# A linear-attention and MLP kernel: a sixth buffer for the k and q features, and a new order of all operations

## The chip, the cores and the metric

The kernel runs on 1 core of a Trainium2 chip. The metric is the device time of one execution in microseconds (us), the median over several runs. The engines are TensorE (PE; its weight loads are listed as PEld), VectorE (DVE), ScalarE (ACT) and GpSimd (POOL); SyncE (SP) issues the DMA transfers. SBUF is the on-chip memory of the engines, PSUM the banks that TensorE writes into.

## What is computed

Eight batches of eight heads of linear attention feed a token-wise MLP, all in fp32:

```
def phi(x):                                   # (8, 8, 576, 64) -> 256 features
    proj = einsum('bhsd,df->bhsf', x, w_phi)  # w_phi 64 x 128
    proj = proj - max(abs(proj), axis=-1)
    return concatenate([exp(proj), exp(-proj)], axis=-1)
q_p, k_p = phi(q), phi(k)
kv  = einsum('bhsf,bhsd->bhfd', k_p, v)
z   = sum(k_p, axis=2)
num = einsum('bhsf,bhfd->bhsd', q_p, kv)
den = einsum('bhsf,bhf->bhs', q_p, z)[..., None] + 1e-6
x   = (num / den) as 4608 tokens x 512

h  = x @ w_in                                 # 512 -> 1024
e  = exp(h - max(h)); sm = e / (sum(e) + 1e-9)
s  = h * sm
ln = (s - mean(s)) / sqrt(var(s) + 1e-6) * g_ln
out = ln @ w_out                              # 1024 -> 512
```

## The kernel before

**Attention.** There are 16 units u (a batch and four of its heads), each with two sub-visits. For a sub-visit TensorE projects k (`k_rows`, `k_mid`: tiles pjk, op name kp) and q (`q_proj`: tiles pq, three products of high and low halves, op name qp with a 320- and a 256-column part; for units 0 to 2 `q2_rows`, tiles pjq). DVE takes the row maximum of k (km) and subtracts it into a feature tile ek (`k_sub`, ks), and ACT makes exp(x) and exp(-x) of it (`k_exp`, ke). The q side is turned by DVE transposes (qt: blk<-pq), has its maximum taken (qm4), is subtracted on POOL (qs), turned back into a feature tile fq (`q_back`, qb), and made into exponentials by ACT (`q_exp`, qe). `visit` (V) then issues on TensorE the 72 num matmuls of the sub-visit before it and the 80 kv matmuls of its own; ACT copies kv out (kvf), the quotient is made (E, rc, y), and y goes by DMA to a scratch tensor dx.

**Tag e.** The tiles ek (four heads by four token blocks) and fq, and the exponential tiles of the last MLP tiles (`moe_tile`, t > 32), take their room from one tag, `e`, with tiles of 5,120 bytes per partition. `SBUF_BUFS` (lines 40 to 43) says how many tiles a tag has.

**MLP.** 36 token tiles t of 128 tokens go in 18 pairs g. The weights w_in come in four loads (wraw, 1 MB each; `w_load`), are rejoined from their 64-bit form by ACT (whi, op ws) and DVE (wb, wd), split into high and low halves (wb_h, wb_l, wt_h, wt_l), and for w_out also scaled (wg) and copied by ACT (w_out_h, op woh). A pair reads x as xT by four DMAs from dx, POOL makes sums S, ACT and POOL split them (ah, al), TensorE makes four shared products U1 to U4 (`moe_shared`) and three own ones (`moe_h`), each of six matmuls, DVE joins them with a running maximum (nm). Each tile then goes through an exponential, a product, a centring and a square pass (eu; op var is the square) to a DVE transpose, a DMA out and four in (du, uTs), a high copy on ACT (uhs), a low part on POOL (uls), and 24 matmuls o in two halves (`moe_o`), and a copy os that goes out.

**What sets the order.** Nothing is scheduled by a cost when the kernel is built: `SEQUENCE` (lines 55 to 192) is a table of 2,604 operation numbers, `Plan.order` walks it, gives each new tile the buffer of its tag that came free first, and the main loop plays the operations in that order. Each engine runs its own instructions in the order of the table, and so does SP its DMA issues. Every instruction is recorded at line 274, in `InOrder`, so the profile tells operations apart by their tiles. PSUM has six banks of tag a and one pair of tag h.

Of the kernel before, what the change touches and what calls it, by code (L numbers as in the profile page):

```python
# [41 lines left out]
    rk=3, rkm=2, rv=3, m=4, e=5, eh=2, kf=2, qr=2, qh=4, q4=2, m4=2, E=2, rc=2,  # L42
# [13 lines left out]
    120, 3, 121, 4, 76, 110, 124, 87, 177, 78, 20, 95, 0, 122, 88, 200, 77, 125, 96, 111, 79, 89, 83, 80, 81,  # L56
    90, 116, 21, 180, 123, 84, 85, 97, 112, 12, 91, 113, 126, 82, 266, 114, 86, 210, 92, 117, 93, 127, 115, 129,
    8, 94, 128, 206, 130, 98, 131, 166, 102, 99, 100, 106, 118, 103, 119, 135, 101, 132, 104, 181, 201, 16, 107,
    178, 22, 105, 133, 152, 134, 155, 137, 182, 146, 136, 23, 108, 13, 153, 58, 59, 157, 183, 156, 154, 14, 202,
    15, 60, 61, 9, 149, 204, 203, 205, 109, 10, 167, 147, 148, 211, 11, 150, 151, 168, 158, 44, 48, 169, 184,  # L60
    214, 17, 45, 170, 159, 173, 186, 255, 212, 138, 171, 174, 216, 160, 269, 213, 219, 18, 56, 57, 62, 289, 172,
    215, 207, 161, 139, 185, 162, 163, 175, 140, 187, 19, 217, 176, 267, 218, 208, 179, 196, 220, 24, 209, 270,
    221, 192, 256, 34, 141, 271, 64, 222, 164, 193, 290, 46, 25, 188, 189, 225, 291, 197, 223, 242, 47, 165,
    194, 224, 257, 142, 343, 195, 190, 227, 226, 292, 243, 268, 6, 228, 35, 244, 275, 272, 354, 377, 229, 191,
    245, 262, 236, 258, 143, 144, 230, 274, 263, 198, 259, 239, 145, 273, 36, 231, 49, 357, 5, 246, 232, 264,
    293, 294, 260, 247, 276, 265, 261, 237, 199, 29, 240, 63, 241, 50, 233, 234, 238, 285, 281, 51, 282, 305,
    378, 7, 379, 66, 248, 249, 250, 299, 277, 52, 26, 283, 235, 251, 308, 358, 54, 27, 295, 296, 286, 306, 359,
    360, 284, 252, 253, 39, 278, 310, 345, 309, 297, 298, 311, 314, 53, 279, 307, 350, 65, 380, 40, 254, 346,
    55, 312, 1410, 351, 280, 1411, 315, 381, 300, 382, 1412, 316, 1413, 313, 28, 67, 301, 302, 287, 352, 30,
    303, 304, 383, 444, 1414, 401, 317, 327, 318, 1418, 1419, 353, 330, 361, 1415, 1424, 31, 41, 42, 1416, 344,  # L70
    68, 1420, 384, 1426, 385, 1475, 1476, 324, 1434, 1477, 1427, 288, 355, 356, 331, 325, 1478, 333, 1421, 1430,
    1417, 37, 362, 329, 326, 1422, 1425, 1428, 425, 347, 32, 328, 33, 402, 1423, 69, 386, 335, 348, 1483, 349,
    1429, 1435, 1479, 332, 436, 1432, 334, 1437, 387, 437, 438, 1480, 1431, 1438, 1441, 1484, 364, 1433, 70,
    319, 71, 369, 38, 365, 1442, 1439, 1443, 370, 373, 1485, 1446, 1436, 1486, 336, 1481, 1447, 1491, 320, 403,
    371, 1482, 374, 366, 337, 72, 1440, 1458, 526, 1444, 439, 388, 321, 1492, 1493, 1448, 372, 391, 483, 1459,
    1494, 1495, 1460, 1496, 1487, 1449, 1450, 404, 405, 427, 392, 367, 406, 1489, 407, 1451, 389, 1488, 432,
    408, 1499, 440, 363, 368, 390, 1497, 433, 393, 459, 1452, 426, 1500, 322, 323, 409, 441, 375, 43, 74, 338,
    73, 1502, 1490, 434, 1463, 442, 394, 1503, 1453, 1464, 1506, 410, 339, 1465, 443, 395, 518, 376, 428, 446,
    1466, 75, 484, 340, 1467, 1507, 1508, 429, 671, 411, 1454, 430, 341, 1511, 342, 435, 431, 485, 1468, 412,
    1445, 1512, 1504, 396, 1513, 460, 415, 413, 397, 1498, 414, 416, 398, 417, 451, 1455, 452, 461, 1501, 1514,  # L80
    1456, 399, 1469, 455, 1515, 1516, 447, 418, 1470, 400, 486, 419, 420, 1505, 1461, 421, 1509, 541, 462, 422,
    448, 449, 450, 445, 1517, 487, 488, 1471, 423, 456, 424, 463, 465, 1540, 453, 542, 1518, 464, 466, 489, 454,
    1541, 1542, 1543, 543, 1462, 1472, 467, 1519, 1473, 490, 1548, 491, 468, 623, 469, 1523, 492, 507, 470, 473,
    1544, 1549, 471, 1545, 544, 545, 1550, 472, 1546, 547, 1551, 1524, 600, 1520, 1525, 1457, 1554, 1556, 546,
    565, 521, 1547, 548, 1564, 1552, 549, 1605, 550, 1558, 1553, 474, 475, 1606, 1607, 1557, 1510, 1555, 508,
    493, 527, 1528, 1559, 519, 1567, 1560, 1521, 1565, 1608, 1609, 1613, 1529, 1530, 1562, 1531, 522, 1526,
    1522, 1561, 1568, 520, 1614, 1571, 1610, 1563, 1532, 494, 495, 1533, 523, 1572, 1569, 457, 476, 477, 528,
    566, 567, 647, 1573, 590, 509, 458, 589, 497, 1576, 1615, 1621, 496, 1577, 1578, 1611, 514, 478, 1579, 498,
    1580, 1612, 1474, 524, 682, 1616, 1566, 1622, 510, 525, 603, 515, 516, 511, 604, 605, 1623, 551, 499, 1625,
    512, 1624, 513, 533, 517, 1581, 534, 1619, 537, 1534, 1527, 1570, 1626, 1620, 1535, 1588, 1536, 1617, 529,  # L90
    1589, 500, 530, 538, 648, 608, 552, 555, 1590, 649, 568, 553, 1593, 569, 535, 536, 501, 479, 1594, 1618,
    591, 556, 571, 570, 557, 480, 572, 1574, 573, 554, 1629, 1582, 1632, 1575, 764, 574, 1537, 1583, 575, 531,
    481, 532, 1630, 1538, 601, 1633, 602, 1591, 592, 1595, 539, 606, 593, 1636, 1592, 1627, 558, 559, 1637, 560,
    482, 1584, 594, 561, 576, 1596, 1597, 595, 579, 562, 1598, 563, 1638, 577, 1634, 607, 1628, 502, 705, 596,
    578, 580, 540, 597, 624, 564, 1631, 503, 581, 625, 1635, 1599, 1585, 504, 598, 599, 619, 505, 683, 1586,
    1600, 1653, 582, 626, 506, 583, 584, 1641, 1639, 629, 1642, 620, 585, 706, 1654, 1655, 586, 587, 1539, 627,
    628, 588, 1670, 630, 610, 1671, 615, 1672, 631, 1601, 632, 1602, 616, 1673, 707, 617, 611, 612, 1678, 609,
    633, 1603, 729, 613, 650, 651, 652, 673, 1674, 1643, 1679, 685, 653, 1644, 614, 1604, 684, 1675, 1680, 1686,
    1684, 1735, 1658, 1694, 1676, 1687, 634, 635, 637, 654, 655, 1659, 1681, 1690, 678, 1677, 1682, 1656, 638,
    1736, 618, 672, 639, 1645, 1683, 656, 1688, 1697, 1660, 1692, 1689, 1695, 730, 1646, 657, 1685, 679, 1640,  # L100
    1691, 1698, 1661, 686, 687, 636, 690, 1647, 1693, 1648, 621, 1701, 1702, 1699, 708, 1737, 674, 680, 1738,
    1739, 1740, 681, 658, 640, 641, 711, 642, 643, 644, 675, 1743, 661, 1744, 691, 731, 754, 709, 1703, 645,
    662, 663, 1741, 710, 712, 1662, 622, 1663, 713, 1706, 1696, 1749, 659, 660, 1649, 676, 1745, 1746, 714,
    1704, 1705, 1664, 1751, 688, 1650, 1752, 1665, 689, 1742, 677, 1700, 1651, 1753, 1755, 811, 812, 715, 1754,
    1756, 701, 1718, 1719, 646, 813, 1707, 732, 1708, 1709, 1710, 664, 665, 753, 692, 1711, 666, 667, 716, 773,
    1720, 717, 668, 1723, 702, 1750, 1666, 1759, 1721, 1747, 1748, 1724, 1712, 1713, 772, 719, 697, 733, 669,
    693, 720, 694, 755, 721, 698, 735, 1762, 670, 1760, 695, 734, 736, 737, 765, 766, 699, 1667, 756, 1587, 757,
    696, 1725, 700, 1722, 1726, 718, 1727, 1728, 703, 1657, 1763, 1766, 738, 758, 759, 1729, 1730, 760, 722,
    1652, 1757, 723, 787, 1767, 1768, 739, 1771, 1769, 1731, 761, 704, 1772, 767, 1773, 724, 1774, 1758, 1668,
    1669, 740, 741, 835, 1764, 742, 743, 1732, 762, 744, 745, 725, 763, 726, 768, 769, 846, 727, 1761, 847, 770,  # L110
    771, 1765, 788, 783, 789, 790, 728, 746, 1775, 747, 1776, 748, 869, 749, 793, 750, 1770, 751, 1733, 1777,
    784, 752, 1778, 1800, 791, 792, 2, 814, 794, 817, 795, 870, 871, 815, 774, 816, 1714, 1801, 818, 796, 1802,
    797, 1783, 1803, 1808, 1809, 1814, 1804, 849, 1734, 1805, 1784, 1785, 819, 850, 893, 894, 1715, 1806, 1807,
    820, 851, 852, 848, 836, 1779, 1788, 917, 1810, 1816, 1865, 1716, 1866, 1811, 1867, 1868, 1786, 821, 1780,
    1781, 1824, 779, 1817, 780, 798, 801, 775, 776, 802, 1818, 1789, 1869, 1812, 1870, 1827, 799, 872, 875,
# [1202 lines left out]
```

## Time and profile before

| | us |
|---|---|
| three runs | 637.32, 641.12, 640.41 |
| median | 640.41 |
| profiled execution | 634.97 |
| its span on the core | 633.2 |

The profiled execution lies 5.44 us under the median of the runs. Its span is divided below into windows of 20 us; the busy time of an engine in a window is the time in which it had an instruction in execution. In the timelines each row gives the start, the duration, the engine, the tiles (out<-in) and the number of instructions put together; brackets hold the idle time before and what ended it.

### The profile page before, as it was taken

To read this page: it belongs to the slowest core of one execution; us is meant where nothing else is said; L and a number is where in the kernel's file an instruction comes from. 1 tells how busy PE (TensorE), PEld (TensorE's weight loads), DVE (VectorE), ACT (ScalarE), POOL (GpSimd) and SP (SyncE) were. 2 spreads that over 40 slices of the span, in tenths; PEclk is the share of its full clock that TensorE was granted. 3 is DMA by queue.
4 is the path that set the end of the run, shared out by engine and by line. 5 is a ranking of instruction groups with operands and counts; after the bars stand their busy time and mean duration, and the time that the engine had idled before them with its cause. 6 is when DMAs were issued, how large, how long until landed. Compare 5 with 4: busy or idle time off the path is not lost.

```text
span 633.2 us, 19010 instructions
## 1 busy us (share of the span) xinstructions
PE 617.8 (98%) x7558; PEld 525.0 (83%) x7558; DVE 475.3 (75%) x995; ACT 458.1 (72%) x842; POOL 432.0 (68%) x468
## 2 busy tenths in 40 slices
PE   6999899999999999999999999999999999999997
PEld 5988688878888888888888888888888888888887
DVE  6999999787868885877876779988897973453540
ACT  4999798677957877477877667887776686466743
POOL 0568998777658864856786586657876675487732
PEclk9999999999999999999999999999999999999999
DMA  8886354754438374455574627545535355356441
GB/s 282 310 274 206 95 162 165 217 144 158 133 115 228 118 218 146 132 143 129 155 229 158 166 87 227 161 126 194 157 128 145 103 165 182 82 158 182 150 134 67
DMA packets 100200, 103.38 MB, mean 163 GB/s; under 512 B 50448, under 2 KB 73232, under 8 KB 99600
## 3 DMA queue, kind: packets, MB, share of 16 engines
q1 hardware_dynamic: 100112, 102.18, 52.8%
q8 instruction: 59, 0.97, 0.6%
q14 instruction: 29, 0.24, 0.1%
HBM read 64.92 MB, written 37.22 MB: 161 GB/s over the span
## 4 chain that ended last, share of the span: by engine, by line
PE 88%; DVE 6%; ACT 2%; DMA 2%; issue 1%; SPq 0%; ACTq 0%; DVEq 0%
PE o L274 31%; PE U L274 15%; PE h L274 12%; PE num L274 10%; PE kv L274 9%; PE pjk L274 5%; PE pq L274 4%; DVE m L274 2%; DVE w L274 1%; DVE ek L274 1%; PE pjq L274 1%; DVE dq L274 1%; DMA xT<-dx 1%; ACT fq L274 1%; DMA out<-os 1%
## 5 line engine op out<-in xcount | busy, mean ns | idle before, releaser
L274 PE MATMUL o<-w_out_h,uhs 128*128 128x512 f32 x280 | 112.4, 402 | 0.0
L274 POOL TENSOR_TENSOR uls<-uTs,uhs 128x1024 fp32r<-128x1024 f32 x35 | 83.7, 2390 | 41.9 <-ACT uhs L274 28.9
L274 PE MATMUL o<-w_out_l,uhs 128*128 128x512 f32 x280 | 109.4, 391 | 0.0
L274 PE MATMUL o<-w_out_h,uls 128*128 128x512 f32 x280 | 109.2, 390 | 0.0
L274 ACT ACTIVATE ek<-ek 128x512 f32<-128x512 f32 (+1 forms) x160 | 90.6, 584 | 16.9 <-DVE ek L274 16.1
L274 PEld LDWEIGHTS num<-kvf,fq 128*64 128x64 f32 x2304 | 70.0, 138 | 9.6 <-issue 5.0
L274 PE MATMUL kv<-rv,ek 128*64 128x65 f32 x2048 | 76.9, 222 | 0.0
L274 PE MATMUL num<-kvf,fq 128*64 128x65 f32 x2304 | 74.4, 223 | 0.1
L274 POOL TENSOR_TENSOR blk<-blk,m 128x1152 f32<-128x1152 f32 x26 | 55.6, 2138 | 27.3 <-DVE m L274 27.3
L274 ACT ACTIVATE fq<-fq 128x640 f32<-128x640 f32 (+1 forms) x104 | 69.4, 679 | 6.1 <-DVE fq L274 5.6
L274 PEld LDWEIGHTS kv<-rv,ek 128*64 128x64 f32 x2048 | 71.0, 138 | 0.8 <-ACT fq L274 0.2
L274 ACT ACTIVATE eu<-h,nm 128x1024 f32<-128x1024 f32 x36 | 40.1, 1115 | 36.4 <-DVE nm L274 31.7
L274 PEld LDWEIGHTS o<-w_out_h,uhs 128*128 128x128 f32 x280 | 52.6, 188 | 12.5 <-issue 0.2
L274 POOL TENSOR_TENSOR al<-S,ah 128x512 fp32r<-128x512 f32 x36 | 47.5, 1320 | 21.8 <-ACT ah L274 20.9
L274 PEld LDWEIGHTS o<-w_out_h,uls 128*128 128x128 f32 x280 | 52.6, 188 | 11.2
L274 PEld LDWEIGHTS o<-w_out_l,uhs 128*128 128x128 f32 x280 | 52.6, 188 | 10.3
L274 POOL TENSOR_TENSOR y<-E,rc 128x512 f32<-128x512 f32 x64 | 43.6, 704 | 21.3 <-DVE rc L274 19.1
L274 DVE TENSOR_REDUCE m<-pjk 128x4 f32<-128x512 f32 (+1 forms) x80 | 48.9, 620 | 11.4 <-PE pjk L274 11.1
L274 DVE SCALAR_TENSOR_TENSOR eu<-h,eu 128x1024 f32<-128x1024 f32 x36 | 43.8, 1218 | 18.1 <-ACT eu L274 17.7
L274 DVE STREAM_TRANSPOSE ub<-eu 128x1024 f32<-128x1024 f32 x35 | 43.1, 1233 | 14.3 <-ACT eu L274 5.5
L274 DVE STREAM_TRANSPOSE blk<-pq 128x320 f32<-128x320 f32 (+1 forms) x104 | 43.4, 455 | 10.8 <-PE pq L274 10.7
L274 POOL TENSOR_TENSOR lq<-rawq,hq 128x576 fp32r<-128x576 f32 x26 | 37.2, 1432 | 20.9 <-ACT hq L274 20.1
(113 smaller groups left out, 1558.4 us busy)
## 6 DMA issues: line engine op xcount, KB each, us to landing
du<-ub SPq DMA_DIRECT2D x35, 512.0 KB, 3.0
uTs<-du SPq DMA_DIRECT2D x140, 128.0 KB, 3.2
dx<-y SPq DMA_DIRECT2D x32, 288.0 KB, 2.7
out<-os SPq DMA_DIRECT2D x35, 256.0 KB, 3.0
rv<-in_v SPq DMA_DIRECT2D x32, 264.0 KB, 4.1
rawk<-in_k SPq DMA_DIRECT2D x32, 256.0 KB, 4.0
xT<-dx SPq DMA_DIRECT2D x64, 128.0 KB, 3.3
rawq<-in_q SPq DMA_DIRECT2D x26, 288.0 KB, 3.9
```

The lines of the kernel that those rows point to most:

```text
L274: return self.tc.keep_in_program_order(method(*args, **kwargs))
```

## The change

Tag `e` gets six tiles instead of five, and `SEQUENCE` is another order of the same 2,604 operations. No operation is added, taken away or changed. Of the 2,604 places 79 hold the same operation as before; half of the operations stand at most 10 places from where they stood, the farthest 742.

```diff
@@ -39,7 +39,7 @@
 SBUF_BUFS = dict(
-    rk=3, rkm=2, rv=3, m=4, e=5, eh=2, kf=2, qr=2, qh=4, q4=2, m4=2, E=2, rc=2,
+    rk=3, rkm=2, rv=3, m=4, e=6, eh=2, kf=2, qr=2, qh=4, q4=2, m4=2, E=2, rc=2,
     y=1, m2k=2, S=2, A=4, A1=2, c=3, big=6, nm=4, sm=3, ms=2, mv=2, sa=2, sc=3,
 )
@@ -53,142 +53,142 @@
 SEQUENCE = (
-    120, 3, 121, 4, 76, 110, 124, 87, 177, 78, 20, 95, 0, 122, 88, 200, 77, 125, 96, 111, 79, 89, 83, 80, 81,
+    3, 120, 0, 76, 87, 4, 95, 121, 77, 124, 96, 116, 78, 88, 110, 90, 122, 89, 125, 20, 83, 84, 206, 117, 85,
...
```

Walked through, the old table holds five e tiles at a time at 20 of the 131 allocations and never asks for more; the new one holds six at 13 of them, the first time in unit 0.

What the table moves, at four places. **SP at the start**, before:

```order
L274 DMA wph<-in_w_phi 128x256
L274 DMA rawk<-in_k 128x512
L274 DMA rawq_155<-in_q 128x512
L274 DMA rawk<-in_k 128x128 x2
L274 DMA wraw_173<-in_w_in 128x2048
L274 DMA rawk<-in_k 128x512
```

and now, later in its list:

```order
L274 DMA rawq_164<-in_q 128x128
L274 DMA vz_70<-in_v 64x132
L274 DMA rawq_177<-in_q 128x512
L274 DMA vz_70<-in_v 64x132
L274 DMA wraw_186<-in_w_in 128x2048
L274 DMA rawq_192<-in_q 128x128
L274 DMA rawk<-in_k 128x128
```

The load of the fourth w_in block (wraw, the first of the four that ACT uses) was SP's seventh DMA and is its twelfth, behind a q load (rawq_177) that needs a tile which an earlier projection frees. On ACT its copy whi stood second after the two w_phi copies and now stands ninth.

**ACT before the visit of unit 3, second half**, before (the last fq row here is the last feature that this visit's num needs; ek and fq are its k and q exponentials):

```order
L274 ACTIVATE fq<-fq 128x2x320
L274 ACTIVATE ek<-ek 128x4x128
L274 ACTIVATE fq<-fq 128x2x320
L274 ACTIVATE fq<-fq 128x2x256
L274 CAST uhs<-uTs 128x1024
L274 ACTIVATE w_7_1257<-w_7_1257,gcol 128x512 x2
L274 CAST w_out_h<-w_7_1257 128x1024
```

and now:

```order
L274 ACTIVATE fq<-fq 128x2x256
L274 ACTIVATE ek<-ek 128x4x128
L274 CAST w_out_h<-w_7_1261 128x1024
L274 ACTIVATE fq<-fq 128x2x320
L274 ACTIVATE ek<-ek 128x4x128
L274 CAST uhs<-uTs 128x1024
L274 ACTIVATE eu,mv<-eu 128x1024 x2
```

The copy w_out_h of the last weight block, and ahead of these rows its scaling, stood behind the features and now stand ahead of the last two of them; the square pass of tile 0 (eu,mv) has moved from ahead to behind.

**PE at the first product U of pair 4**, before:

```order
L274 MATMUL pq<-hq,w_hh 128x320 x2
L274 MATMUL pq<-hq,w_ll 128x320 x2
L274 MATMUL pq<-lq,w_hh 128x320 x2
L274 MATMUL pjk<-wph,rawk 128x128 x8
L274 MATMUL pjk<-wph,rawk 128x256
L274 MATMUL pq<-hq,w_hh 128x256 x2
L274 MATMUL pq<-hq,w_ll 128x256 x2
L274 MATMUL pq<-lq,w_hh 128x256 x2
L274 MATMUL U<-wb_h,ah 128x512
L274 MATMUL U<-wb_l,ah 128x512
```

and now:

```order
L274 MATMUL o<-w_out_h,uhs 128x512
L274 MATMUL o<-w_out_l,uhs 128x512
L274 MATMUL o<-w_out_h,uls 128x512
L274 MATMUL pjk<-wph,rawk 128x128 x8
L274 MATMUL pq<-hq,w_hh 128x256 x2
L274 MATMUL pq<-hq,w_ll 128x256 x2
L274 MATMUL pq<-lq,w_hh 128x256 x2
L274 MATMUL U<-wb_h,ah 128x512
L274 MATMUL U<-wb_l,ah 128x512
L274 MATMUL U<-wb_h,al 128x512
```

Ahead of U now stand the second half of an o, a projection pjk and one part pq only; the other pq part and the small pjk have moved ahead of that o half.

**PE after the visit of unit 14, second half**, where the q projections of unit 15 stand, before:

```order
L274 MATMUL pq<-hq,w_hh 128x256 x2
L274 MATMUL pq<-hq,w_ll 128x256 x2
L274 MATMUL pq<-lq,w_hh 128x256 x2
L274 MATMUL pq<-hq,w_hh 128x320 x2
L274 MATMUL pq<-hq,w_ll 128x320 x2
L274 MATMUL pq<-lq,w_hh 128x320 x2
L274 MATMUL pjk<-wph,rawk 128x128 x8
L274 MATMUL h<-wt_h_1023,ah 128x512
```

and now:

```order
L274 MATMUL pq<-hq,w_hh 128x320 x2
L274 MATMUL pq<-hq,w_ll 128x320 x2
L274 MATMUL pq<-lq,w_hh 128x320 x2
L274 MATMUL pjk<-wph,rawk 128x128 x8
L274 MATMUL pq<-hq,w_hh 128x256 x2
L274 MATMUL pq<-hq,w_ll 128x256 x2
L274 MATMUL pq<-lq,w_hh 128x256 x2
L274 MATMUL o<-w_out_h,uhs 128x512
```

Before, the 320-column part of unit 15's first sub-visit stood ahead of the visit, its 256-column part behind the visit and the second sub-visit's 320-column part directly behind that. Now both parts of the first sub-visit stand behind the visit with the eight k projections between them, and the second sub-visit's parts come behind the products o of tile 24.

## Rows read from the trace of the kernel before

**Rows 1.** The page: busy time of each engine with its share of the span and its instructions.

```profile
PE 617.8 (98%) x7558; PEld 525.0 (83%) x7558; DVE 475.3 (75%) x995; ACT 458.1 (72%) x842; POOL 432.0 (68%) x468
```

**Rows 2.** Busy time by windows: from:to and length, then for each engine the busy time and (instructions), the granted clock, the share of the DMA engines in use and GB/s.

```profile
0.00:20.00 20.00, 14.45 (x184) 12.31 (x185) 13.87 (x25) 11.30 (x24) 1.24 (x9) 1.00 0.88 307
20.00:40.00 20.00, 19.01 (x400) 16.63 (x400) 19.26 (x31) 18.43 (x40) 14.39 (x10) 1.00 0.78 271
40.00:60.00 20.00, 18.59 (x398) 16.31 (x397) 18.05 (x30) 19.20 (x47) 16.66 (x14) 1.00 0.70 225
60.00:80.00 20.00, 17.84 (x266) 15.04 (x266) 18.88 (x29) 15.27 (x32) 19.82 (x13) 1.00 0.46 121
80.00:100.00 20.00, 20.00 (x337) 17.45 (x334) 17.59 (x36) 19.96 (x36) 18.67 (x15) 1.00 0.50 165
100.00:120.00 20.00, 19.65 (x253) 16.43 (x248) 16.10 (x39) 16.18 (x32) 15.85 (x17) 1.00 0.55 175
120.00:140.00 20.00, 19.05 (x140) 15.21 (x141) 17.70 (x46) 11.53 (x20) 16.70 (x22) 1.00 0.73 192
...
480.00:500.00 20.00, 19.40 (x305) 16.43 (x305) 18.22 (x43) 12.48 (x24) 10.11 (x15) 1.00 0.30 82
...
560.00:580.00 20.00, 20.00 (x90) 16.58 (x89) 9.96 (x18) 12.76 (x19) 16.02 (x20) 1.00 0.58 167
```

**Rows 3.** Waits: the instruction that waited, what it waited for, us in total, times, the longest. First those of PE, then the only one of all engines in which a new ek or fq waited for its buffer.

```profile
PE pjq L274 <- DMA wph<-in_w_phi: 3.8, 1, 3.8
PE U L274 <- DVE blk L274: 2.2, 1, 2.2
...
DVE ek L274 <- PE kv L274: 1.8, 2, 1.6
```

**Rows 4.** The start, timeline of SP's queue: the first and the last of the four loads of w_in blocks (1 MB each).

```profile
3.52 0.44 SPq L274 DMA_DIRECT2D wraw<-in_w_in  x1
...
15.76 0.70 SPq L274 DMA_DIRECT2D wraw<-in_w_in  x1
```

**Rows 5.** The DMA view of the moments 3.5 and 15.7 us: the wraw load issued there, KB, us from issue to landing.

```profile
wraw<-in_w_in SPq DMA_DIRECT2D x1, 1024.0 KB, 7.2
...
wraw<-in_w_in SPq DMA_DIRECT2D x1, 1024.0 KB, 8.7
```

**Rows 6.** The start, timeline of ACT: the copy of the first loaded block, and what stands at the place that is ninth in its list.

```profile
10.74 1.07 ACT L274 ACTIVATE whi<-wraw 128x1024 f32<-128x1024 f32 x1 [0.18 <-DMA wraw<-in_w_in]
...
14.22 0.41 ACT L274 ACTIVATE ek<-ek 128x256 f32<-128x256 f32 x1
```

**Rows 7.** Timelines of PE and of POOL around the first product U.

```profile
68.40 0.47 PE L274 MATMUL U<-wb_h,ah 128*128 128x512 f32 x1 [2.15 <-DVE blk L274]
...
65.09 1.72 POOL L274 TENSOR_TENSOR al<-xT,ah 128x512 fp32r<-128x512 f32 x1
...
69.20 2.21 POOL L274 TENSOR_TENSOR al<-S,ah 128x512 fp32r<-128x512 f32 x1
```

**Rows 8.** Timeline of ACT before and behind the visit of unit 3, second half: square pass, the last features, the scaling and copy of the last weight block, and the last features of the next visit.

```profile
87.16 1.05 ACT L274 ACTIVATE eu<-eu 128x1024 f32<-128x1024 f32 x1
...
93.25 1.25 ACT L274 ACTIVATE fq<-fq 128x640 f32<-128x640 f32 x2
...
95.34 1.34 ACT L274 ACTIVATE w<-w,gcol 128x512 f32<-128x512 f32 x2
96.71 1.05 ACT L274 CAST w_out_h<-w 128x1024 fp32r<-128x1024 f32 x1
...
106.27 2.69 ACT L274 ACTIVATE fq<-fq 128x640 f32<-128x640 f32 x4
```

**Rows 9.** Timeline of PE in the same stretch: the visit's start, the projection behind it, and the next visit's start.

```profile
95.72 2.32 PE L274 MATMUL num<-kvf,fq 128*64 128x65 f32 x72
...
101.14 1.16 PE L274 MATMUL pjk<-wph,rawk 64*128 64x128 f32 x14 [0.35 <-DVE m L274]
...
109.26 1.92 PE L274 MATMUL num<-kvf,fq 128*64 128x65 f32 x58
```

**Rows 10.** Timelines of PE and ACT around the first product U of pair 4.

```profile
191.28 0.41 PE L274 MATMUL pq<-hq,w_hh 64*128 64x320 f32 x2
...
191.82 1.68 PE L274 MATMUL pjk<-wph,rawk 64*128 64x128 f32 x18
193.71 0.39 PE L274 MATMUL pq<-hq,w_hh 64*128 64x256 f32 x2 [0.20 <-ACT os L274]
...
194.26 0.50 PE L274 MATMUL U<-wb_h,ah 128*128 128x512 f32 x1
...
192.45 0.62 ACT L274 CAST ah<-xT 128x512 fp32r<-128x512 f32 x1 [1.56 <-DMA xT<-dx]
```

**Rows 11.** Timeline of PE behind the visit of unit 14, second half.

```profile
486.12 0.78 PE L274 MATMUL pq<-hq,w_hh 64*128 64x256 f32 x2
...
486.75 0.39 PE L274 MATMUL pq<-lq,w_hh 64*128 64x256 f32 x2
487.71 0.42 PE L274 MATMUL pq<-hq,w_hh 64*128 64x320 f32 x2 [0.58 <-DVE c L274]
...
488.26 1.05 PE L274 MATMUL pjk<-wph,rawk 64*128 64x128 f32 x16
489.24 0.50 PE L274 MATMUL h<-wt_h,ah 128*128 128x512 f32 x1
```

270 rows, old and new, of the table SEQUENCE are left out of this document.

## The prediction

> **What bounds the kernel now.** I read the page first: PE is busy for 617.8 of 633.2 us [rows 1], so only 15.4 us of the span are free of TensorE work, and the change neither adds nor removes a matmul. Then the windows, which show where these 15.4 us lie: 5.55 in 0 to 20 us, 0.99, 1.41 and 2.16 in the next three, 0 in 80 to 100, 0.35 and 0.95 up to 140, and 0.60 in 480 to 500 [rows 2]; nearly all of the rest is the fill and drain of the last microseconds. From 0 to 140 that makes 11.4 us. In this first stretch the others are full in turn: DVE 19.26, 18.05 and 18.88 of 20 in the windows from 20 to 80, ACT 19.20 and 19.96 in those from 40 and 80, POOL 19.82 in that from 60 [rows 2]. Behind 140 PE itself is the limit and the others have room, as in 560 to 580 with DVE at 9.96 and ACT at 12.76 [rows 2]. The granted clock is 1.00 in all of these windows, the upper level of 2.4 GHz. Third come the waits: the longest of PE is 3.8 us for w_phi at the start, the next 2.2 before the first U, and only twice, for 1.8 us together, does a new ek wait for a tile of tag e to come free [rows 3].
>
> So the sixth buffer relieves a wait of 1.8 us, on DVE, in a program that TensorE bounds; what the change is worth has to come from the order.
>
> **The change part by part.** The sum is made against the profiled execution, 634.97 us, which is 5.44 under the median of 640.41; I add the sum to the median.
>
> *PE's work.* The same matmuls; fewer changes between kinds of block (2,156 rows in the order instead of 2,161) are nothing I can tell. 0.
>
> *The sixth buffer.* Walked through, it is held at 13 places, so it is used. Its whole price in the trace is 1.8 us of DVE idle [rows 3], in a stretch where DVE is 90 to 96% busy with work that comes afterwards all the same. 0 on PE's path by itself, -1.8 at most.
>
> *The start.* The first w_in load was issued at 3.52 us and landed 7.2 later; ACT's copy of it came at 10.74 and had waited 0.18 for it [rows 4 to 6]. It now stands behind a q load that needs a tile which the first projections free, and ACT's copy is ninth, where ACT stands at 14.22 [rows 6]. An issue at about 7 us, an estimate from those projections (they end near 6), with the 7.2 of the same load gives 14.2: no wait. With the 8.7 of the last load [rows 5] and an issue at 8.9 it would land at 17.6 and ACT would wait 3.4 us; ACT's list runs in order, so its exponentials wait as well. I take 0, since the same block at nearly the same moment has the 7.2; ends 0 and +3.4. POOL's list has room here (1.24 of 20 busy [rows 2]).
>
> *The first U.* Its 2.15 us wait is put down to a DVE transpose that frees a PSUM bank [rows 7]. The new table gives it a bank that an earlier transpose frees. But the product also needs its low part al from POOL, 65.09 to 66.81, and the later products need the next al, which ended at 71.41 and which the table puts behind one more POOL sum; POOL has 0.18 us free in this window [rows 2, 7]. What U gains it is likely to wait for again. 0; ends -1.6 (68.40 less 66.81) and +1.2 (one more sum and its wait).
>
> *80 to 110 us.* ACT is full, 19.96 of 20 [rows 2]. The visit of unit 3, second half, started at 95.72, and the last features it needed first ended at 94.50, a slack of 1.2 [rows 8, 9]. The scaling and the copy of the last weight block, 1.34 and 1.05, now stand ahead of the last of them, and a square pass of 1.05 goes behind: +1.3 against 1.2 of slack, so next to nothing here. Up to the next visit's last features, which ended at 108.96 for a start at 109.26, a slack of 0.3 [rows 8, 9], these moves cancel, but the square pass of the following tile, another 1.05, has come in ahead of them: 1.05 less 0.3 is about +0.7. A wait of PE before a projection (0.35 shown at 101.14, and the block is late by about 1.1 as a whole [rows 9]) goes, because that projection moves behind the o; but a PE that is earlier finds ACT no earlier. I take +0.7; ends -1.1 (only the gain) and +2.0 (both sets of ACT work fall on PE).
>
> *The first U of pair 4.* It hung on xT: ACT's cast waited 1.56 us for the DMA and started at 192.45 [rows 10]. PE spent the time on 18 projections that took 191.82 to 193.71, 1.89 us, where 16 take 0.98 [rows 11] and the two of double width would add a quarter of that; the excess is about 0.66, in which the wait of 0.20 lies [rows 10]. Now half an o stands in that place, and the U comes about 1.85 us of PE work later. -0.7; ends -0.9 and 0. The U's consumers come later too, on DVE and ACT, whose lists have room here.
>
> *Behind unit 14.* The two pq groups back to back took 486.12 to 488.26, and the second waited 0.58 for the bank that a DVE addition frees [rows 11]. Where nothing waits, one group takes 0.54 (191.28 to 191.82 [rows 10]); so 2.14 less 1.08 is 1.06 of excess. With eight projections between them and DVE's transposes done meanwhile I take -1.0; ends -1.06 and 0. DVE is the fullest engine beside PE here, 18.22 of 20 [rows 2], so what could be late next is the row maximum behind those projections; an o of 2.7 us covers it.
>
> *The rest of the table*, 140 to 480 and 500 to 633: pieces of DVE and POOL work move by one to two microseconds against PE, in windows where PE is 20.00 of 20 busy and DVE has two to ten free. 0.
>
> Sum: 0 + 0 + 0 + 0.7 - 0.7 - 1.0 = -1.0. The profiled execution comes to 634.0, the median to **639.4 us**, no change. The ends without the buffer's are -4.7 and +6.6, all of them at once.
>
> **The rivals.** A measurement of this kernel can tell about 1%, 6.4 us, from no change: faster means under 634.0, slower over 646.8.
>
> *The first 140 us open up.* With room for features ahead and a new order, PE's idle time there goes: 11.4 less the 3.8 of the w_phi load, which no buffer shortens, is 7.6 [rows 2, 3]; with -1.7 from the two later places, 640.4 - 9.3 = 631.1 us. For it: the gaps come again and again in this stretch, and the start has been rearranged most. Against it: DVE, ACT and POOL are full in turn, and a buffer makes none of them faster. The Trainium skill (Perfetto Trace Analysis, Optimization Strategy) says that the same gap repeating on the engine that should be saturated can mean that there is not enough SBUF for the next tile; by that rule the 7.6 us would go. Here the trace disagrees: the gaps of PE name w_phi, a transpose and an addition, and the e tile is named for 1.8 us on DVE. Chance 0.18.
>
> *ACT falls behind.* The late first load holds ACT's list for 3.4 us at its ninth place. From 20 to 100 ACT has 1.6, 0.8, 4.7 and 0.04 us free per window [rows 2], but what it makes there is waited for; the 3.4 reach the visit at 109, where the slack is 0.3 and 1.05 more stand ahead. Then 640.4 + 3.4 + 0.7 = 644.5 us if the later places give nothing, 642.8 if they do, and one microsecond more for each that the load lands behind 17.6. It decides when the load lands after 14.2. For it: the DMA engines are 0.88 busy in the first window [rows 2], and three of the four w_in loads stand later in SP's list, and ACT makes the copies in a fixed order. Against it: the same load took 7.2 [rows 5], and POOL, which uses the blocks, has spare time until 60. Chance 0.17, of which 0.11 beyond 646.8.
>
> *Nothing but noise.* The buffer's wait is off the path and the other gains are given back where the next thing is late: 640.4. Chance 0.05.
>
> *PE is not full.* Its weight loads are busy for 525.0 us, 83% [rows 1]. The Trainium skill (Perfetto Trace Analysis, Identifying the Most-Contended Engine) holds that matmul busy time is a poor measure of headroom and weight-load busy time a better one; by that there would be up to 108 us to win. Where PE never waits, in 560 to 580, it shows 20.00 of 20 beside 16.58 of weight loads, which is also 83% [rows 2], so that share is what a fed PE looks like. Chance below 0.01.
>
> **How the numbers follow.** Forecast 0.60, opening up 0.18, ACT behind 0.17, noise 0.05. Faster by over 1% is the first rival, 0.18; slower is the far part of the second, 0.11; within 1% is the rest, 0.71. The range for 8 in 10 starts at 632.0, which leaves out the better half of the first rival, about 0.09, and ends at 646.5, which leaves out 0.11.
>
> **What would show it.** In the profile after: w_in's first copy on ACT at about 14 us with little or no wait; the wait before the first U shorter and PE's busy time in 60 to 80 still near 17.8; PE's start of the visits at 95.7 and 109.3 later by no more than a microsecond; no 0.58 wait behind unit 14; PE at 20.00 in the windows from 140 on; no wait on the e tag. A PE busy time well above 19 in the windows from 20 to 80 would be the first rival, an ACT wait for wraw of over a microsecond the second. What would make it wrong is above all the first 110 us, where three engines change their order at once and I priced only the places at which a wait stands now.

## The result: 1.0% slower, and the profile after

The change takes 644.4 us (median of 15 runs, 641.3 to 646.18) against 638.61 us before (15 runs, 636.01 to 641.12). The ratio is 1.0101, 95% interval 1.0083 to 1.0118. Here and below a ratio is estimated from the single runs outside the chip's slower state, so it is not the quotient of the two medians. The prediction had 639.4 us and a gain too small to tell; it was wrong in sign and size.

The profiled execution took 643.35 us with a span of 641.6, 8.4 us more than the profiled execution of before, which lay 3.6 under the median of its runs. Its page, engines and granted clock, answers to [rows 1]:

```profile
PE 619.8 (97%) x7558; PEld 525.9 (82%) x7558; DVE 471.1 (73%) x995; ACT 458.2 (71%) x842; POOL 432.3 (67%) x468
...
PEclk9999998999999999999899999999999999999999
```

The work is the same, instruction for instruction. But two of the 40 slices of the clock are not full, where before every window had 1.00 [rows 2]. The windows of 20 us in which PE lost most show where to look (columns as in [rows 2]):

```profile
60.00:80.00 20.00, 17.00 (x222) 13.35 (x219) 18.84 (x32) 16.71 (x34) 20.00 (x14) 1.00 0.52 139
80.00:100.00 20.00, 16.21 (x193) 13.69 (x188) 16.52 (x34) 17.24 (x31) 18.34 (x14) 0.94 0.44 147
...
220.00:240.00 20.00, 18.91 (x246) 16.10 (x245) 17.12 (x39) 15.92 (x28) 12.43 (x12) 1.00 0.69 216
...
300.00:320.00 20.00, 17.90 (x131) 14.39 (x126) 14.28 (x31) 12.90 (x25) 13.14 (x16) 0.91 0.62 184
...
560.00:580.00 20.00, 18.46 (x82) 14.99 (x81) 9.73 (x17) 11.63 (x19) 15.75 (x21) 1.00 0.52 161
```

Before, PE had 17.84 in the first of these windows and 20.00 in the other four. PE's waits name the reason; the kind that cost 1.0 us in one place before now costs 6.9 in four:

```profile
PE h L274 <- DVE nm L274: 6.9, 4, 3.8
PE pjq L274 <- DMA rawq<-in_q: 4.4, 1, 4.4
PE U L274 <- DVE c L274: 2.1, 1, 2.1
PE U L274 <- POOL al L274: 1.8, 1, 1.8
```

The longest stands at 93 us. PE's timeline there, the last projection and the next product:

```profile
91.95 1.05 PE L274 MATMUL pjk<-wph,rawk 64*128 64x128 f32 x16
96.79 0.47 PE L274 MATMUL h<-wb_h,ah 128*128 128x512 f32 x1 [3.79 <-DVE nm L274]
```

and DVE's at the same time:

```profile
91.36 1.24 DVE L274 STREAM_TRANSPOSE ub<-eu 128x1024 f32<-128x1024 f32 x1
92.52 1.20 DVE L274 STREAM_TRANSPOSE blk<-pq 128x320 f32<-128x320 f32 x3
93.65 0.65 DVE L274 TENSOR_REDUCE m<-pjk 128x4 f32<-128x512 f32 x1
94.22 0.43 DVE L274 STREAM_TRANSPOSE blk<-pq 128x256 f32<-128x256 f32 x1
94.58 0.65 DVE L274 TENSOR_TENSOR ek<-pjk,m 128x512 f32<-128x512 f32 x1
95.15 0.67 DVE L274 TENSOR_REDUCE m<-pjk 128x4 f32<-128x512 f32 x1
95.75 0.24 DVE L274 RECIPROCAL rc<-rc 128x18 f32<-128x18 f32 x1
95.92 0.67 DVE L274 CUSTOM_DVE_ANT_0 h<-h,c 128x512 f32<-128x512 f32 x1
```

The product that waits is the second one of pair 1, `moe_h` with i = 1, which writes columns 512 to 1023 of the tile h (call it h1). What it waits for is `moe_join` with i = 0 (join 0), which reads and writes columns 0 to 511 of the same tile. They share no column. But in the table join 0 now stands ahead of h1, and DVE reaches join 0 only behind nine other instructions, three of which (m, ek, m) belong to the projection that PE made last. In the table before, h1 of this pair stood ahead of join 0. I looked at all 18 pairs in the traces of before, of the change and of the mended order below: join 0 and h1 of a pair never run at the same time. Whichever stands first in the table is over (by 0.03 us or more) when the other starts, 54 times out of 54.

In this execution the clock falls behind two of the waits. Windows over the stretches behind 96 and behind 312 us, the granted clock third from the end:

```profile
96.00:101.00 5.00, 4.21 (x12) 3.30 (x12) 3.04 (x6) 3.65 (x7) 4.52 (x4) 0.66 0.43 132
...
312.00:316.00 4.00, 4.00 (x12) 3.09 (x12) 3.28 (x8) 2.41 (x5) 2.26 (x3) 0.57 0.79 217
```

Of 5.0 us a third is lost, and of 4.0 us 0.43, 1.7 us each. The four waits of the mechanism at pairs 1, 5, 16 and 17 are 3.79, 1.09, 2.10 and 1.54, together 8.5 us; with the clock 11.9. (Of the four waits of h in the list above three are these, at pairs 1, 5 and 17; the fourth, 0.47 at pair 0, is left out here. The wait at pair 16 is the 2.1 us of U for c.) The span grew by 8.4, so some 3.5 us came back elsewhere.

A changed order of the two is not the price by itself. By the two tables nine of the 18 pairs have join 0 and h1 the other way round, and PE waits at three of these only, pairs 0, 1 and 16. At pairs 5 and 17 join 0 stood ahead of h1 before as well; DVE comes to it later now. At pair 5 in the kernel before join 0 was over 0.63 us ahead of h1, and now three m and three ek stand directly ahead of it:

```profile
232.66 1.84 DVE L274 TENSOR_REDUCE m<-pjk 128x4 f32<-128x512 f32 x3
234.54 1.89 DVE L274 TENSOR_TENSOR ek<-pjk,m 128x512 f32<-128x512 f32 x3
236.34 0.69 DVE L274 CUSTOM_DVE_ANT_0 h<-h,c 128x512 f32<-128x512 f32 x1
```

The wait of pair 16 (2.10 us at 311.70) is the same relation the other way round. Here h1 stands first; DVE's list:

```profile
309.75 0.70 DVE L274 CUSTOM_DVE_ANT_0 h<-h,c 128x512 f32<-128x512 f32 x1 [2.56 <-PE h L274]
...
310.97 0.68 DVE L274 TENSOR_TENSOR c<-U,c 128x512 f32<-128x512 f32 x1
```

Join 0 holds DVE for 2.56 us until h1 is over, the addition into c stands behind it, and that addition frees the PSUM bank that PE's next U needs.

### The profile page after: what moved, and what is told of

Same layout as the page of the kernel before. It is cut to its first block, busy times and chain, and to the rows that moved or that the text cites. A ratio compares the mean times of both kernels' runs of the same rounds, so it can differ in the third digit from the quotient of the medians.

```text
span 641.6 us, 18952 instructions
## 1 busy us (share of the span) xinstructions
PE 619.8 (97%) x7558; PEld 525.9 (82%) x7558; DVE 471.1 (73%) x995; ACT 458.2 (71%) x842; POOL 432.3 (67%) x468
## 4 chain that ended last, share of the span: by engine, by line
PE 85%; DVE 6%; ACT 3%; DMA 2%; POOL 2%; issue 1%; SPq 0%; POOLq 0%; ACTq 0%; DVEq 0%
PE o L274 31%; PE U L274 15%; PE h L274 11%; PE num L274 10%; PE kv L274 9%; PE pjk L274 4%; PE pq L274 4%; DVE m L274 2%; DVE w L274 1%; ACT ek L274 1%; DMA dx<-y 1%; DVE ek L274 1%; ACT fq L274 1%; POOL w_out_l L274 1%; DMA xT<-dx 1%
## 5 line engine op out<-in xcount | busy, mean ns | idle before, releaser
L274 DVE STREAM_TRANSPOSE blk<-pq 128x256 f32<-128x256 f32 (+1 forms) x104 | 43.6, 454 | 12.7 <-PE pq L274 12.5
L274 DVE TENSOR_TENSOR ek<-pjk,m 128x512 f32<-128x512 f32 (+1 forms) x80 | 48.8, 623 | 3.6 <-PE kv L274 2.7
```

The source lines that it names most:

```text
L274: return self.tc.keep_in_program_order(method(*args, **kwargs))
```

## The experiments

The theory (A): a pair's join 0 and its h1 exclude each other in the order of the table, so that a late engine stops the other one; the loss of the change is these waits and the low clock behind them. Rivals: (B) the engines are full there, and PE would wait for the next thing instead; (C) the sixth buffer itself costs. In the edits below the numbers of the table are operations; the traces of these kernels show line 278 for 274, because their tables take more lines.

### The old order with six tiles

```diff
-    rk=3, rkm=2, rv=3, m=4, e=5, eh=2, kf=2, qr=2, qh=4, q4=2, m4=2, E=2, rc=2,
+    rk=3, rkm=2, rv=3, m=4, e=6, eh=2, kf=2, qr=2, qh=4, q4=2, m4=2, E=2, rc=2,
```

> The order of before with six e tiles instead of five. Theory A (the wait of h for a join that the new table puts ahead of it makes the loss): the buffer alone costs nothing, 1.00 of before within 0.3%, and the start of every visit stays where it was within 0.5 us. Rival C (the sixth buffer itself costs, by its place in SBUF or by earlier writes): about 1.01 of before, the loss of the change.

Measured: 638.29 us against 637.16, ratio 1.0003 (0.9983 to 1.0022). The buffer alone neither costs nor gives. Rival C is out.

### Two neighbours exchanged (join 0 is 1502, h1 is 1500)

```diff
-    432, 339, 1502, 1500, 430,
+    432, 339, 1500, 1502, 430,
```

> The changed kernel with two neighbours of the table exchanged: pair 1's second product h now stands ahead of the first join of the same pair, and nothing else moves. Theory A: the 3.8 us wait of PE for DVE at 93 us goes, and with it the stretch of low clock behind it (four microseconds of matmuls at 0.43 instead of 0.23 apart, 1.5 to 2 us): 4 to 6 us faster than the change, 638 to 640 us. Rival B (DVE and ACT are full in this stretch, and PE would wait for the features of the next visit instead): within 1 us of the change, the wait standing at the num of unit 3, second half.

Measured: 638.56 against 637.16, ratio 1.0018 (1.0000 to 1.0036); the change has 1.0101, so 0.83% or 5.3 us came back from one exchange. PE's timeline at the place, where in the change h followed 3.79 us late:

```profile
93.75 1.05 PE L278 MATMUL pjk<-wph,rawk 64*128 64x128 f32 x16
94.73 0.50 PE L278 MATMUL h<-wb_h,ah 128*128 128x512 f32 x1
...
97.70 2.32 PE L278 MATMUL num<-kvf,fq 128*64 128x65 f32 x72
```

The visit behind (num) starts at 97.70 instead of 101.30, with no wait of its own: rival B is out at this place.

### The join earlier instead of later

```diff
-    1496, 1488, 372, 1463,
+    1496, 1502, 1488, 372, 1463,
...
-    432, 339, 1502, 1500, 430,
+    432, 339, 1500, 430,
```

> The changed kernel with pair 1's first join moved forward in the table, to behind the additions into c that end at 91.4 us, so that it still stands ahead of the product h but no longer behind seven other DVE operations. Theory A, in the form that the wait is DVE's lateness passed on by the order of the two: the join ends near 92, h does not wait, and the gain over the change is the same 4 to 6 us as from the exchange, about 1.002 of before. If a join ahead of h costs something by itself, wherever DVE stands: less than half of it.

Measured: 637.93 against 637.29, ratio 1.0011 (0.9996 to 1.0026), as the exchange. On DVE join 0 now runs at

```profile
93.20 0.69 DVE L278 CUSTOM_DVE_ANT_0 h<-h,c 128x512 f32<-128x512 f32 x1
```

and no wait is left there. So a join ahead of its h1 costs nothing while DVE is on time; the price is DVE's lateness, handed to PE.

### Pair 16 alone (the addition is 1896, h1 is 1902, join 0 is 1904)

```diff
-    1895, 1840, 1902, 1904, 882, 884, 1841, 1854, 924, 1944, 1842, 1843, 1896, 859,
+    1895, 1840, 1896, 1902, 1904, 882, 884, 1841, 1854, 924, 1944, 1842, 1843, 859,
```

> The changed kernel with one operation moved: pair 16's first addition into c, which frees the bank that the product U waits for, now ahead of that pair's first join on DVE, which has to wait for h. Theory A (a join and the product h of the same pair hold each other up as the table orders them): the 2.1 us wait of PE at 310 us and the low clock behind it go, 3 to 4 us faster than the change, 640 to 641.5 us. Rival B (PE waits at the next operation instead): within 1 us of the change.

Measured: 640.95 against 637.92, ratio 1.0042 (1.0026 to 1.0058), 0.59% or 3.8 us better than the change. That equals the wait of 2.10 and the 1.7 us of low clock behind it, but the agreement is luck: in the profile of this run a wait of 0.46 us stays at the place and one of 1.03 us is new further on. The estimate under "The clock" below puts most of the gain down to the clock.

```profile
311.16 0.50 PE L278 MATMUL U<-wt_h,ah 128*128 128x512 f32 x1 [0.46 <-DVE blk L278]
...
353.83 0.50 PE L278 MATMUL o<-w_out_h,uls 128*128 128x512 f32 x1 [1.03 <-POOL uls L278]
```

### The mended order: pairs 1, 5, 16 and 17

```diff
-    432, 339, 1502, 1500, 430,
+    432, 339, 1500, 1502, 430,
...
-    758, 1762, 737, 835, 767, 1729, 1760, 738,
+    758, 737, 835, 767, 1729, 1760, 1762, 738,
...
-    1840, 1902, 1904, 882, 884, 1841, 1854, 924, 1944, 1842, 1843, 1896, 859,
+    1840, 1896, 1902, 1904, 882, 884, 1841, 1854, 924, 1944, 1842, 1843, 859,
...
-    2428, 2436, 2374, 2422, 2434, 2383, 2430, 2437,
+    2428, 2374, 2422, 2434, 2383, 2430, 2436, 2437,
```

> As swap1, and the same exchange for pairs 5 and 17, and for pair 16 the addition into c, which frees the bank that U waits for, put ahead of the join that waits for h. Theory A: a further 1.1, 1.5 and 2.1 us of waits go with their low clock: 8 to 12 us faster than the change in all, 633 to 637 us, faster than before. Rival B: at most 2 us faster than the change, new waits at the operations behind these.

Measured: 632.56 us against 637.16, ratio 0.9920 (0.9896 to 0.9944): 1.81% or 11.5 us faster than the change by moving four operations, and 0.8% faster than before. The profiled span is 630.2, 11.4 less than the change's, where the waits and the clock added up to 11.9. PE's waits:

```profile
PE pjq L278 <- DMA rawq<-in_q: 4.1, 1, 4.1
PE U L278 <- POOL al L278: 1.8, 1, 1.8
...
PE h L278 <- DVE nm L278: 0.4, 1, 0.4
```

### The wait put into the kernel before

In the old order three operations of pair 1 and behind it, join 0 (1502), h1 (1500) and the next visit (375), are put behind a DVE transpose (1463), join 0 first.

```diff
-    1452, 426, 1500, 322, 323, 409, 441, 375, 43, 74, 338, 73, 1502, 1490, 434, 1463, 442,
+    1452, 426, 322, 323, 409, 441, 43, 74, 338, 73, 1490, 434, 1463, 1502, 1500, 375, 442,
```

> The kernel before with one thing of the change put in: pair 1's first join stands ahead of h in the table, and behind a transpose of 1.25 us on DVE. Theory A: PE waits about 2 us for the join at 94 us and the time rises by 2 to 4 us over before, more than the wait if the clock falls after it. Rival B: within 1 us of before, since ACT's features end at 94.5 anyway and its work behind is unchanged.

Measured: 640.2 against 637.16, ratio 1.0040 (1.0020 to 1.0059), 2.5 us slower. The wait came as asked for:

```profile
96.59 0.50 PE L278 MATMUL h<-wb_h,ah 128*128 128x512 f32 x1 [2.13 <-DVE nm L278]
```

In this profile the clock stayed at 1.00 behind it; at 636.9 us it is the fastest of the twelve executions, so it does not show what the others lost. By the estimate under "The clock" 0.8 us of the loss are wait and 1.4 clock.

### Needless matmuls in the wait

Thirty, and then fifteen, matmuls of two identity blocks into a spare bank between the projection and h1 of pair 1. Nothing reads what they write.

```diff
+    def fill():
+        w = bank("a", [P, 512], "fill")
+        for _ in range(30):
+            nc.tensor.matmul(w[:, :P], lhsT=ident, rhs=ident, start=True, stop=True)
+    op("fill", "tensor", 0, 0, fill, (), [(4, "kp", 0)], [("a", "fill")])
```

> The changed kernel with 30 needless 128x128 matmuls put on PE where it waits 3.8 us for the join of pair 1; they write a spare bank and nothing reads them. The wait for the join stays as it is. If the low clock behind the wait comes from the pause and is a cost of its own: the matmuls behind it stay 0.23 us apart, the granted clock of that window is 1.00 and the kernel is 1.5 to 2 us faster than the change. If the clock falls for another reason, or if the low stretch costs nothing because ACT is late there: same as the change within 0.5 us.

> The changed kernel with 15 needless 128x128 matmuls in PE's 3.8 us wait of pair 1 (30 of them took 6.7 us in the run before and so outlasted the wait; 15 should take about 3.4). The wait itself stays. If the low clock behind the wait is a cost of its own and comes from the pause: the matmuls behind it 0.23 us apart and 1 to 2 us faster than the change, near 1.008 of before. If that low stretch is hidden by ACT: same as the change, 1.010.

Measured: with thirty 647.12 against 637.92, ratio 1.0132 (1.0092 to 1.0172). They took 6.7 us, nearly twice the wait (each call is two instructions of 0.11 us), so the run says nothing of the price of the clock. With fifteen 642.53 against 637.29, ratio 1.0063 (1.0038 to 1.0088), 0.38% or 2.4 us better than the change; the interval of each of the two is about a quarter of a per cent to either side, so the gain is shown and its size is rough. Its PE:

```profile
95.32 3.61 PE L278 MATMUL fill<-ident 128*128 128x128 f32 x30
99.06 0.47 PE L278 MATMUL h<-wb_h,ah 128*128 128x512 f32 x1
...
100.50 0.39 PE L278 MATMUL U<-wt_h,ah 128*128 128x512 f32 x1
100.73 0.39 PE L278 MATMUL U<-wt_l,ah 128*128 128x512 f32 x1
```

h1 still starts 3.8 us behind the projection's end, but the matmuls behind it follow each other at 0.23 us at once, the upper level of 2.4 GHz; the window from 99 to 104 us has a granted clock of 1.00. One execution does not settle it: in the profile of the kernel with pair 16 alone mended the pause of pair 1 is just as long and empty, and the clock behind it is full too (1.00 from 98 to 103 us):

```profile
98.06 0.47 PE L278 MATMUL h<-wb_h,ah 128*128 128x512 f32 x1 [3.79 <-DVE nm L278]
...
98.00:103.00 5.00, 4.94 (x80) 4.21 (x82) 3.57 (x10) 4.34 (x10) 3.78 (x4) 1.00 0.58 140
```

The timed runs decide. The mean granted clock over whole executions is 0.991 for the change (15 runs) and 0.996 with the pause filled (10 runs). On a span of 641 us this is 3.0 us, and 2.4 came back. So a pause makes the low clock more frequent, not certain, and the low clock is a cost beside the wait. The Trainium skill (TensorE: Matmul & The Clock Gate, Part 1: The HAM clock gate) says that the low rate is the default and that activity of the engine releases it. The runs agree with it on the average only: behind the filled pause the profile has 1.00, behind the empty one 0.66 in one execution and 1.00 in another.

### The mended order with five tiles

The operations that found no free e tile, and those that hang on them, come later in the table; the first of them, in unit 0:

```diff
-    rk=3, rkm=2, rv=3, m=4, e=6, eh=2, kf=2, qr=2, qh=4, q4=2, m4=2, E=2, rc=2,
+    rk=3, rkm=2, rv=3, m=4, e=5, eh=2, kf=2, qr=2, qh=4, q4=2, m4=2, E=2, rc=2,
...
-    210, 147, 156, 24, 154, 135, 148, 289, 129, 204, 151, 22, 205, 180, 202, 150, 207, 157, 108, 136,
+    210, 156, 24, 154, 135, 289, 204, 22, 205, 129, 202, 157, 180, 136,
...
-    137, 168,
+    137, 108, 147, 148, 151, 150, 168,
```

> The mended order (four exchanges) played with five e tiles: the operations that found no tile, and those that depend on them, come later in the table, which moves the last features of unit 0 and of unit 1 and the two visits they share tiles with. If the sixth buffer is what the order lives from: slower than the mended order by 1 us or more, with the loss before 60 us. If it only relieved 1.8 us of DVE idle: within 1 us of the mended order, 631 to 634 us.

Measured: 671.4 against 637.92, ratio 1.0503 (1.0464 to 1.0542). By the start of unit 2's second half 6 us are lost against the mended order, and PE then waits in many other places, up to 550 us. So this order lives from the sixth tile. The granted clock fell as well, to 0.976 in the mean, which by the estimate below is 15.9 us of span against 2.2 in the runs of before beside it. It doesn't follow that no order with five tiles is as good: I only let operations wait in this one, and the kernel before is an order with five.

### The al of pair 0 ahead of a sum on POOL

```diff
-    288, 1417, 32, 36, 1420, 1421, 42,
+    288, 32, 36, 1420, 1421, 1417, 42,
```

> The mended order, and for pair 0 the low part al that the second shared product waits for put ahead of the third sum S on POOL, as it stood before the change. Theory A: the wait of 1.8 us of U for al at 70 us goes: 1 to 1.8 us faster than the mended order. Rival B: POOL is full there (20.0 of 20), the third sum and what hangs on it come later and PE waits at h instead: within 0.5 us.

Measured: 633.2 against 637.92, ratio 0.9922 (0.9901 to 0.9943), the same as the mended order. The wait of U for al fell from 1.82 to 0.17 us and came back at h of the same pair:

```profile
71.06 0.50 PE L278 MATMUL U<-wt_h,al 128*128 128x512 f32 x1 [0.17 <-POOL al L278]
...
76.29 0.47 PE L278 MATMUL h<-wb_h,ah 128*128 128x512 f32 x1 [2.12 <-DVE nm L278]
```

Here rival B is right: with POOL and DVE full, one wait taken away shows the next.

### The new start with the old rest, and one exchange in the old order

The first kernel has six tiles; its table begins with the first 311 operations of the new one, up to unit 2's second visit, and goes on with all others in the old order. The second, whose edit is the last one below, moves join 0 of pair 2 (1567) behind its h1 (1565) in the kernel before.

```diff
-    rk=3, rkm=2, rv=3, m=4, e=5, eh=2, kf=2, qr=2, qh=4, q4=2, m4=2, E=2, rc=2,
+    rk=3, rkm=2, rv=3, m=4, e=6, eh=2, kf=2, qr=2, qh=4, q4=2, m4=2, E=2, rc=2,
...
-    120, 3, 121, 4, 76, 110, 124, 87, 177, 78, 20, 95, 0, 122, 88, 200, 77, 125, 96, 111, 79, 89, 83, 80, 81,
+    3, 120, 0, 76, 87, 4, 95, 121, 77, 124, 96, 116, 78, 88, 110, 90, 122, 89, 125, 20, 83, 84, 206, 117, 85,
```

```diff
-    1559, 519, 1567, 1560, 1521, 1565, 1608,
+    1559, 519, 1560, 1521, 1565, 1567, 1608,
```

> Six e tiles, the new order up to the visit of unit 2, second half (about 59 us), and behind that the old order of all that is left. If the first 60 us of the new order are a gain of their own (PE reaches that visit 1.2 to 1.5 us earlier in the profiles): 0.5 to 1.5 us faster than before. If what is gained there is given back at the full engines behind it (60 to 100 us): same as before within 0.5 us.

> The kernel before with one exchange: pair 2's first join behind the product h of the same pair. Theory A: PE's wait of 1.0 us for that join at 134 us goes: 1 us faster than before, 0.998. Rival B (waits at the next operation): same as before.

Measured: the new start 635.84 against 637.29, ratio 0.9971 (0.9953 to 0.9990), 1.8 us faster. In its profile the visit of unit 2's second half starts 1.3 us earlier than before (58.97 for 60.24) and the next two only 0.5 (78.30 for 78.79, 95.26 for 95.72), so most of the head start is given back. What its timed runs have is a higher clock, 0.9995 in the mean against 0.9975 for before, which is 1.3 us; why it is higher stays open. The exchange took 637.39 against 637.29, ratio 0.9991 (0.9964 to 1.0019), no difference that can be told. In the latter the wait of h is gone, and PE waits for the same engine one operation later:

```profile
PE pq L278 <- DVE nm L278: 1.2, 1, 1.2
```

## Why the prediction was wrong

**The step that failed** is the rule by which I chose what to price: only the places at which a wait stands in the trace of before. In the words of the prediction, "*The rest of the table* ... 0" and the +0.7 for 80 to 110 us. At pairs 5, 16 and 17 the rest of the table brought 1.09, 2.10 and 1.54 us of wait and 1.7 of low clock; in 80 to 110 us the visits that started at 95.72 and 109.26 [rows 9] start at 101.30 and 114.00, 5.6 and 4.7 us later. At pair 1 the table turned round the order of join 0 and h1. I had compared what each operation needs as data, and these two share none; I had not asked which pairs of operations of different engines write one tile, which of the two comes first, and how late its engine is there. Both orders are in the table before, with waits of at most 1.0 us, because DVE was on time there; DVE's other work behind which a join is put decides the price. The bound of +2.0 for that stretch was too small for the same reason, and the range ended at 646.5 only because of a rival whose mechanism did not happen. That 644.4 lies inside the range is luck, and so is that the second rival's sum, 644.5, meets it.

**The clock.** No term had it. With 3.4 us in the profiled execution it is more than a quarter of the 11.9. In the 15 timed runs of the change it was never full: the run with 0.997 took 641.3 us, the seven runs with 0.989 took 644.72 to 646.18.

Over the timed runs its part is larger. An estimate: the span of a run times its mean granted clock is the span at full clock, and the rest of the span is what the clock cost. (It charges the whole low stretch to the time, also where PE would have waited for another engine; for the profiled execution it gives 3.2 where the two windows give 3.4.) In microseconds, mean of the runs:

| kernel | runs | mean clock | span at full clock | cost of the clock |
|---|---|---|---|---|
| before (beside the mended order) | 29 | 0.997 | 634.0 | 1.7 |
| the change | 15 | 0.991 | 637.0 | 5.5 |
| two neighbours exchanged | 12 | 0.996 | 634.5 | 2.4 |
| pair 16 alone | 10 | 0.996 | 636.5 | 2.8 |
| pause filled, fifteen matmuls | 10 | 0.996 | 637.7 | 2.5 |
| mended order | 6 | 0.998 | 629.3 | 1.5 |
| the wait put in before | 12 | 0.995 | 634.8 | 3.1 |
| new start, old rest | 12 | 0.9995 | 634.0 | 0.3 |

So the change lost 3.0 us net to its order and 3.8 to the clock, and each edit that takes away or fills one of its two longest pauses gets back about 3 us of clock. The runs of before beside these kernels cost 1.4 to 2.2 us of clock, so the comparison between them is good to about a microsecond.

**The steps that held.** *The sixth buffer*: 0, measured 1.0003. The sign I gave for it, no wait on the e tag, did not come: ek's waits for an e tile are 2.7 us in all now, against 1.8 [rows 3]:

```profile
DVE ek L274 <- PE kv L274: 2.7, 2, 1.6
```

The first rival's rule on the room in SBUF would have given 7.6 us; the old order with a sixth tile gave none. *The start*: no wait for the first w_in block. ACT's copy stands at 13.91 us, where I had 14.2, with no idle time before it:

```profile
13.91 1.12 ACT L274 ACTIVATE whi<-wraw 128x1024 f32<-128x1024 f32 x1
```

So the second rival (ACT behind) did not happen, and the kernel is slower on another path than the one that I gave for it. The visit of unit 2's second half came 1.5 us earlier (60.24 before, 58.70 now), but nothing of that is left at the next one (below). The new start alone gave 1.8 us when timed; at full clock the table has 634.0 for it as for before, so no idle time of PE went, which is what the first rival was about; the gain is in the clock. *The first U*: it came at 64.46 instead of 68.40 [rows 7], and the next U gave it back, by the wait for al that I had named and one for ACT:

```profile
69.32 0.50 PE L274 MATMUL U<-wt_h,ah 128*128 128x512 f32 x1 [0.72 <-ACT c L274]
...
71.86 0.50 PE L274 MATMUL U<-wt_h,al 128*128 128x512 f32 x1 [1.81 <-POOL al L274]
```

The visit behind it starts at 78.92 (78.79 before). *Behind unit 14*: -1.0; the two pq groups and the projections between them now run from 493.56 without a pause, and the stretch from one visit to the next is 1.2 us shorter after taking off the PE work that moved in or out of it:

```profile
493.56 0.41 PE L274 MATMUL pq<-hq,w_hh 64*128 64x320 f32 x2
...
494.11 1.05 PE L274 MATMUL pjk<-wph,rawk 64*128 64x128 f32 x16
494.92 0.36 PE L274 MATMUL pq<-hq,w_hh 64*128 64x256 f32 x2
```

*The first U of pair 4*: -0.7; by the same reckoning -0.5. *ACT in 80 to 110 us*: the +0.7 did not show. In the kernel with the one exchange the visit starts at 97.70, right behind the product before it, so ACT's extra copies were covered; the wait I had put there was DVE's, at another operation.

What stays open: how much of the 3.5 us that came back in the change, and of the 0.8% of the mended order, belongs to which move. By the starts of its visits the mended order is 0.4 us ahead of before at the visit of 109 us, 1.6 at the next (136.64 for 138.28), 2.2 at that of 481 and 3.1 at that of 522, so the gain lies behind 109 us; PE work that moved across a visit is in these numbers. The two places above account for 1.7 by the profile; the others were not tried one by one.

## What to carry to other kernels

When an order written out by hand is replaced, list for every tile that two engines write which of them now comes first, also where they touch different columns of it, and ask what stands ahead of that one in its engine's list. Ask it also where the two kept their order: the list of what has changed places would have missed pairs 5 and 17. A wait that no trace has shown yet is priced by how late the other engine runs at that place, not by zero. On a kernel that TensorE bounds, put work that is ready into a pause, or move the pause's cause: over the timed runs the low clock cost this change more than its order did net of what came back. And compare the granted clock of two sets of runs before a small gain is put down to the order.

## What was not expected of the hardware

The length of a pause alone did not tell whether the clock falls. In the change's profile it fell behind waits of 3.79 us (to 0.66 over the next five microseconds) and of 2.10 us (to 0.57 over four), and stayed at 1.00 behind 1.54 and 1.09; in the kernel before with the wait put in it stayed at 1.00 behind 2.13 us. Nor did the same pause in the same place: behind the 3.79 us of pair 1 it stayed at 1.00 in the profile of pair 16 alone, behind the 2.10 us of pair 16 it stayed at 1.00 in that of the two neighbours exchanged, and behind the 2.15 us before the first U, where the profile of before has 1.00 from 60 to 80 us, the old order with six tiles has 0.91. In the timed runs the clock varied with the same program, 0.989 to 0.997 for the change and 0.994 to 1.000 for 29 runs of the kernel before, which spread from 634.73 to 641.47 us.
